# Packed attention with a SoLU layer: batch 1's Z from float16 halves, and a new order of steps after the first key product

## The chip, the core and the metric

The kernel runs on one core of a Trainium2 chip. The metric is the time of one execution in device microseconds (us), taken on the device; shown is the median of three timed runs. A profile is a separate execution, recorded instruction by instruction. Engines are called PE (TensorE, matrix products), DVE (VectorE), ACT (ScalarE), POOL (GpSimd) and SP (SyncE, which issues nearly all transfers here). PEld is the load of PE's stationary operand, which runs beside PE's products.

## The reference

There are 8 batches with 8 heads, 576 tokens, a head dimension of 64 and 32 packed rows. All tensors are float32.

```python
def sm_attn(qq, kk, vv):
    s = scale * np.matmul(qq, kk.transpose(0, 1, 3, 2))
    s = s - np.max(s, axis=-1, keepdims=True)
    a = np.exp(s)
    a = a / (np.sum(a, axis=-1, keepdims=True) + 1e-09)
    return np.matmul(a, vv)
p_packed = sm_attn(p, k, v)
out = sm_attn(q, p_packed, p_packed)

# x: out with the heads side by side, 4608 tokens x 512
h = x @ w_in                                    # 512 -> 1024
h_max = np.max(h, axis=-1, keepdims=True)
e = np.exp(h - h_max)
sm = e / (np.sum(e, axis=-1, keepdims=True) + 1e-09)
solu = h * sm
mu = np.mean(solu, axis=-1, keepdims=True)
var = np.mean((solu - mu) ** 2, axis=-1, keepdims=True)
ln = (solu - mu) / np.sqrt(var + 1e-06) * g_ln
return (ln @ w_out).astype(np.float32)          # 1024 -> 512
```

## The kernel before

**Flows and their order.** The program is written as generators, called flows, each of which emits its instructions step by step and yields in between. One long string, ORDER, names the flow that takes its next step. Every engine runs its instructions in the order in which they are emitted, so ORDER sets by hand what stands behind what on each engine and on SP's queue. The names in it: lp, lg, lw, lo, lk, lq, lv load p, g_ln, w_in, w_out, k, q, v; W and O take the sizes and scaled halves of w_in and w_out; Z and X issue PE products whose result nobody uses (warm_up, and keep_clock in pairs of L125 products); N, S, C, H are weight_size, w_out_scale, scaled_parts and weight_halves; k*b*, q*b*, z*b* are pack, unpack and make_z of batch *b*; t*i* is token_tile *i*.

**What a batch does.** Pack takes k and v to the packed rows: PE transposes or DVE block transposes of k (L369, L376, L383), scores (L399), maximum on DVE (L403), exponential e on ACT (L406), transposes of e on PE (L422) that are copied to SBUF as e1T (L424), the product with v (L432), and ppT, the packed rows transposed (L448). Unpack takes q to the attention weights a, in float16 halves a_h and a_l: scores (L504, L516), block transposes (L477), the softmax's maximum, difference, exponential, sum, reciprocal and product (L481 to L496), and the halves (L527, L530, L532). The attended rows are never formed: make_z multiplies the packed rows by w_in first, Z = packed rows times w_in, and splits Z into float16 halves zh and zl. Batches 0 and 1 do that in float32 (L570); batches 2 to 7 multiply halves of the packed rows (pph, L549 to L553) by halves of w_in (L564), three products in the place of one.

**What a token tile does.** 4608 tokens are 36 tiles of 128. An even batch and the odd one behind it have four tiles each and share one of the rest (tiles 4, 13, 22, 31). A tile is h = a times Z in 12 float16 products (L631), the negated maximum nm on DVE (L634), its scaled form on ACT (L639), a bound and s_row on POOL (L642 to L648), the exponential on ACT (L652), u = e times h on DVE (L656), negmu on ACT (L660), halves of u plus negmu on ACT (L665) and DVE (L667), a transposing transfer to yT on SP's queue (L670), the square on ACT (L673), small factors on POOL (L676 to L683), 24 output products (L691) and the scaled copy o_sb on ACT or DVE (L697, L699), which SP stores (L708).

**Space.** PSUM has three buffers h of two banks each, which score products, transposes, Z and the tiles' h take in turn, and one each of po and pa. There are three raw buffers for k and q, and one of v (v_sb). A product that takes a buffer waits until the reader of the one before it is done.

**Who does what.** Letter tables choose the engine, p for POOL, d for DVE, a for ACT, for one batch, piece or tile each: SCALED_BY the low part wcl of w_out's scaled halves (L305 to L313; g is POOL), A2L_BY a_l, SOFT_BY the difference and the product of the softmax, LOW_BY the low bits of the weights (L240 to L250), QT_BY and E1T_BY the copies of q's and e's transposes. ZP_BY says with 1 which batches make Z from halves. The line numbers here and in the rows are those of this kernel.

## Time and profile before

| | |
|---|---|
| median of three timed runs | 389.76 us (389.49 to 390.9) |
| profiled execution, own time | 390.44 us |
| its span, first to last instruction | 388.6 us |
| PE busy | 373.8 us, 96% |
| DVE busy | 294.3 us, 76% |
| ACT busy | 256.7 us, 66% |
| POOL busy | 244.8 us, 63% |
| mean granted PE clock | 0.995 |

The own time is 1.8 us longer than the span: that is what lies around the recorded instructions. The profiled execution is 0.68 us above the median. The shares are means over the whole span; the stages differ, so the views by stretch say more. "Idle before" in a row is the time in which the engine waited for the instruction, with what released it.

### The profile page before, as it was taken

The page shows a single profiled execution, that of the slowest core. Times are in us where ns is not written, and L with a number is a line of the kernel's source. Part 1 is how long each engine was busy: PE and PEld are TensorE (multiplying, and loading weights), DVE is VectorE, ACT ScalarE, POOL GpSimd, SP SyncE. Part 2 cuts the span into 40 slices and gives each one's busy share as a digit, 9 for nine tenths or more (in the row PEclk, how much of TensorE's full clock was granted, in tenths as well). Part 3 has the DMA queues.
Part 4 walks back from the last instruction along what each step waited for, and adds up shares of the span by engine and source line. Part 5 has one row for each costly group of instructions (what it writes and reads, how often), then busy time and mean ns, then how long its engine had stood idle before and what let it go on. Part 6 is the DMA issues. An engine that isn't in the chain of part 4 may idle for free.

```text
span 388.6 us, 8528 instructions
## 1 busy us (share of the span) xinstructions
PE 373.8 (96%) x3234; PEld 190.9 (49%) x3234; DVE 294.3 (76%) x472; ACT 256.7 (66%) x447; POOL 244.8 (63%) x410
## 2 busy tenths in 40 slices
PE   6978979999999999999999999999999999999996
PEld 6856435444545444544454455444444444444444
DVE  2577888999987987778798589977777968466631
ACT  2566799795878678955767657754658559465730
POOL 2674689887438987764555476875456658854550
PEclk9989999999999999999999999999999999999999
DMA  8999894898899999999697878873632435353561
GB/s 310 385 375 355 195 213 89 201 167 183 150 228 166 201 215 172 175 180 230 143 199 145 204 142 189 189 167 67 128 81 59 107 108 83 83 132 86 83 162 54
DMA packets 213017, 66.10 MB, mean 170 GB/s; under 512 B 192872, under 2 KB 206960, under 8 KB 212464
## 3 DMA queue, kind: packets, MB, share of 16 engines
q1 hardware_dynamic: 212976, 65.56, 74.4%
q8 instruction: 25, 0.41, 0.5%
q14 instruction: 16, 0.13, 0.1%
HBM read 37.23 MB, written 9.44 MB: 120 GB/s over the span
## 4 chain that ended last, share of the span: by engine, by line
PE 71%; DVE 4%; DMA 2%; ACT 1%; POOL 1%; issue 1%; SPq 0%; DVEq 0%; ACTq 0%
PE po L691 37%; PE h L631 19%; PE h L691 5%; PE h L564 2%; PE pa L432 2%; PE h L399 2%; PE h L516 1%; DMA yT<-yhl 1%; PE h L422 1%; DMA raw<-in_q_dram 1%; DVE u L656 1%; DVE w_in_sb L344 1%; DVE nm L634 1%; ACT e L652 1%; DVE s L477 0%
## 5 line engine op out<-in xcount | busy, mean ns | idle before, releaser
L691 PE MATMUL po<-wch,yT 128*128 128x512 f16 x512 | 160.1, 379 | 0.1
L691 PEld LDWEIGHTS <-yT 128*128 128x128 f16 x888 | 85.8, 98 | 100.6 <-issue 5.3
L691 PE MATMUL po<-wcl,yT 128*128 128x512 f16 x256 | 97.0, 379 | 0.0
L656 DVE SCALAR_TENSOR_TENSOR u<-e,s_row,h 128x1024 f32<-128x1024 f32 x36 | 45.8, 1271 | 18.3 <-ACT e L652 12.9
L667 DVE SCALAR_TENSOR_TENSOR yhl<-u,negmu,yhl 128x1024 f16<-128x1024 f32 x36 | 47.5, 1319 | 4.7 <-ACT yhl L665 4.6
L634 DVE TENSOR_REDUCE nm<-h 128x1 f32<-128x1024 f32 x36 | 43.5, 1212 | 8.3 <-PE h L631 7.9
L631 PE MATMUL h<-zh,a_h 128*128 128x512 f16 (+2 forms) x168 | 47.7, 380 | 0.7 <-ACT qT L371 0.7
L631 PE MATMUL h<-zl,a_h 128*128 128x512 f16 (+2 forms) x168 | 47.9, 380 | 0.0
L631 PEld LDWEIGHTS <-a_h 128*128 128x128 f16 (+2 forms) x336 | 27.7, 100 | 34.6 <-issue 5.2
L652 ACT ACTIVATE e<-h,nmc,z_scale 128x1024 f32<-128x1024 f32 x36 | 43.2, 1201 | 1.9 <-PE h L631 0.8
L665 ACT ACTIVATE yhl<-u,negmu 128x1024 f16<-128x1024 f32 x36 | 41.1, 1145 | 0.7
L673 ACT ACTIVATE e<-u,negmu 128x1024 f32<-128x1024 f32 x36 | 40.9, 1137 | 0.0
L639 ACT ACTIVATE nmc<-nm,z_scale 128x1 f32<-128x1 f32 x33 | 9.6, 292 | 45.9 <-DVE nm L634 45.9
L642 POOL TENSOR_SCALAR bound<-nm,z_scale 128x1 f32<-128x1 f32 x33 | 12.9, 390 | 37.6 <-DVE nm L634 36.1
L680 POOL TENSOR_SCALAR c_row<-sq,s_eps 128x1 f32<-128x1 f32 x36 | 12.8, 355 | 29.3 <-ACT e L673 26.4
L631 PE MATMUL h<-zh,a_l 128*128 128x512 f16 (+2 forms) x84 | 30.4, 379 | 0.1
L631 PE MATMUL h<-zl,a_l 128*128 128x512 f16 (+2 forms) x84 | 30.4, 379 | 0.0
L699 DVE TENSOR_SCALAR o_sb<-po,c_row,inv 128x512 f32<-128x512 f32 x18 | 14.6, 810 | 13.8 <-PE po L691 6.9
L681 POOL TENSOR_TENSOR c_row<-c_row,neg_half 128x1 f32<-128x1 f32 x36 | 22.5, 626 | 3.0
L660 ACT ACTIVATE negmu<-su 128x1 f32<-128x1 f32 x36 | 7.2, 200 | 25.5 <-DVE u L656 25.4
L496 POOL TENSOR_TENSOR a<-a,sm 128x576 f32<-128x576 f32 x16 | 20.3, 1274 | 4.9 <-DVE sm L494 4.3
L532 POOL TENSOR_TENSOR a_l<-s,a_h 128x576 f16<-128x576 f32 x14 | 20.4, 1460 | 4.5 <-ACT a_h L530 4.5
(173 smaller groups left out, 687.8 us busy)
## 6 DMA issues: line engine op xcount, KB each, us to landing
out_dram<-o_sb SPq DMA_DIRECT2D x34, 256.0 KB, 2.3
v_sb<-in_v_dram SPq DMA_DIRECT2D x8, 1024.0 KB, 8.3
raw<-in_k_dram SPq DMA_DIRECT2D x24, 288.0 KB, 4.4
raw<-in_q_dram SPq DMA_DIRECT2D x96, 72.0 KB, 2.5
zh<-in_moe_w_in_dram SPq DMA_DIRECT2D x2, 1024.0 KB, 8.0
zl<-in_moe_w_in_dram SPq DMA_DIRECT2D x2, 1024.0 KB, 7.9
raw<-in_k_dram SPq DMA_DIRECT2D x2, 1024.0 KB, 12.2
raw<-in_moe_w_out_dram SPq DMA_DIRECT2D x2, 1024.0 KB, 8.4
```

Of the source, the lines that this page charges most:

```text
L496: EN(nc, SOFT_BY[2 * b + 1]).tensor_tensor(out=w2, in0=w2, in1=sm.unsqueeze(2).broadcast_to([P, NB, J]), op=ALU.mult)
L532: EN(nc, A2L_BY[2 * b + r]).tensor_tensor(out=lo, in0=a2T, in1=hi, op=ALU.subtract)
L631: nc.tensor.matmul(dst_[:, cols], lhsT=lhsT, rhs=z[:, r, cols], start=bool(first), stop=bool(last))
L634: nc.vector.tensor_reduce(out=nm, in_=h, axis=AX.X, op=ALU.max, negate=True)
L652: nc.scalar.activation(e, h, AF.Exp, bias=nmc, scale=sc[:, 1:], accum_out=se)
L656: nc.vector.scalar_tensor_tensor(out=u, in0=e, scalar=s_row, in1=h, op0=ALU.mult, op1=ALU.mult, accum_out=su)
L665: nc.scalar.activation(yhl[:, 0], u, AF.Identity, bias=negmu)
L667: nc.vector.scalar_tensor_tensor(out=yhl[:, 1], in0=u, scalar=negmu, in1=yhl[:, 0], op0=ALU.add, op1=ALU.subtract)
L673: nc.scalar.activation(e, u, AF.Square, bias=negmu, accum_out=sq)
L681: nc.gpsimd.tensor_tensor(out=c_row, in0=c_row, in1=neg_half, op=ALU.pow)
L691: nc.tensor.matmul(po[:, cols], lhsT=yT[:, a, c], rhs=w[:, c, cols], start=c == 0 and t == 0, stop=c == NFC - 1 and t == 2)
L699: nc.vector.tensor_scalar(out=o_sb[:, cols], in0=po[:, cols], scalar1=c_row, scalar2=inv, op0=ALU.mult, op1=ALU.mult)
```

## The change

Five things change.

- ZP_BY: batch 1's Z is made from the float16 halves, like batches 2 to 7, with 48 float16 products in the place of 16 float32 ones. Its weight halves (H) must therefore be ready before z1, where they had to be ready before z2. The packed rows of batch 1 get halves as well.
- Tables: three of eight wcl parts go from POOL to DVE, a_l on DVE goes from two to seven of 16 pieces, softmax steps on DVE from two to eight of 32 (the table has now an entry for each half of a batch), three copies (two of e1T, one of q1) from ACT to DVE, and the low bits of O2 and O3 from ACT to POOL.
- warm_up yields between its products, which are the same and stand in the same place.
- weight_halves can put its subtraction on POOL; HL_BY puts all four on DVE, as before.
- ORDER is new from the first key product on. Among much else, three pairs of keep_clock's products stand behind the first token tile's h product, and q rows of batch 2 are loaded ahead of batch 1's v.

```diff
-SCALED_BY = 'gggggggg'
+SCALED_BY = 'ggdgdgdg'
-A2L_BY = 'ddpppppppppppppp'
-SOFT_BY = 'ppppppppdppppppp'
-LOW_BY = 'appapaaa'
+A2L_BY = 'pdpppdpddppdddpp'
+SOFT_BY = 'pppdpppppppppppdddppppdppdpdpppd'
+LOW_BY = 'appapapp'
...
-QT_BY = 'dadaaaaaaaaaaaa'
-E1T_BY = 'aaaaaa'
+QT_BY = 'dadaaaaaadaaaaa'
+E1T_BY = 'aaaaaaadaaadaaaa'
...
-ZP_BY = '00111111'
+ZP_BY = '01111111'
...
+HL_BY = 'dddd'
...
@@ warm_up @@
-        for _ in range(24):
-            nc.tensor.matmul(spare[:, :P], lhsT=ones_f, rhs=ones_f, start=True, stop=True)
...
-        yield
+        for _ in range(6):
+            for _ in range(4):
+                nc.tensor.matmul(spare[:, :P], lhsT=ones_f, rhs=ones_f, start=True, stop=True)
+            yield
...
@@ weight_halves @@
-            nc.vector.scalar_tensor_tensor(out=halves[1][g], in0=w_in_sb[:, g], scalar=s_w, in1=halves[0][g], op0=ALU.mult, op1=ALU.subtract)
+            if HL_BY[g] == 'd':
+                nc.vector.scalar_tensor_tensor(out=halves[1][g], in0=w_in_sb[:, g], scalar=s_w, in1=halves[0][g], op0=ALU.mult, op1=ALU.subtract)
...
@@ pack @@
-            copy_by(nc, E1T_BY[2 * b + i0 // 8] if b < 3 else 'a')(e1T[:, i0:i0 + len(grp)], pt[:, :len(grp) * P].rearrange('p (i j) -> p i j', j=P))
+            copy_by(nc, E1T_BY[2 * b + i0 // 8])(e1T[:, i0:i0 + len(grp)], pt[:, :len(grp) * P].rearrange('p (i j) -> p i j', j=P))
...
@@ unpack @@
-            EN(nc, SOFT_BY[2 * b]).tensor_tensor(out=s2[r], in0=s2[r], in1=mx.unsqueeze(2).broadcast_to([P, NB, J]), op=ALU.subtract)
+            EN(nc, SOFT_BY[4 * b + r]).tensor_tensor(out=s2[r], in0=s2[r], in1=mx.unsqueeze(2).broadcast_to([P, NB, J]), op=ALU.subtract)
...
-            EN(nc, SOFT_BY[2 * b + 1]).tensor_tensor(out=w2, in0=w2, in1=sm.unsqueeze(2).broadcast_to([P, NB, J]), op=ALU.mult)
+            EN(nc, SOFT_BY[4 * b + 2 + r]).tensor_tensor(out=w2, in0=w2, in1=sm.unsqueeze(2).broadcast_to([P, NB, J]), op=ALU.mult)
```

Of ORDER the diff is one line of some 1,290 steps, so three places of it are shown as the engines see them. Behind a name stands the number of its buffer. The lines of the kernel after are 4 higher than before up to weight_halves and 8 higher behind it.

PE ahead of the first token tile, before: the last two of z0's four product groups (L570), transposes of k1 and q1 (L369, L376), fillers (L125), the two score products of k1 (L399) and the first weight load of the tile.

```order
L570 MATMUL h_488<-w_in_sb_84,ppT_419 32x512 x4
L125 MATMUL po_120<-ones_98 128x384 x2
L376 MATMUL h_588<-ident_91,raw_470 128x128 x2
L125 MATMUL po_120<-ones_98 128x384 x2
L399 MATMUL h_597<-kT_509,pT_82 32x288 x8
L369 MATMUL h_622<-ident_91,raw_521 128x128 x8
L399 MATMUL h_642<-kT_509,pT_82 32x288 x8
L369 MATMUL h_661<-ident_91,raw_521 128x128 x8
L125 MATMUL po_120<-ones_98 128x384 x2
L631 LDWEIGHTS a_h0_116
L631 MATMUL h_672<-zh_486,a_h0_116 128x512
```

The same place after (L578 is z0's product, L377 and L384 are transposes, L129 the filler, L407 the score product, L639 the tile):

```order
L377 MATMUL h_551<-ident_91,raw_470 128x128 x8
L281 MATMUL pa_564<-ssq_89,ones_f_96 128x8
L384 MATMUL h_578<-ident_91,raw_470 128x128 x2
L129 MATMUL po_120<-ones_98 128x384 x2
L407 MATMUL h_597<-kT_509,pT_82 32x288 x8
L407 MATMUL h_614<-kT_509,pT_82 32x288 x8
L129 MATMUL po_120<-ones_98 128x384 x2
L377 MATMUL h_642<-ident_91,raw_631 128x128 x8
L377 MATMUL h_658<-ident_91,raw_631 128x128 x8
L639 LDWEIGHTS a_h0_116
L639 MATMUL h_667<-zh_489,a_h0_116 128x512
```

Both score products of k1 now stand next to each other, ahead of both transposes of q1, so that with three h buffers the tile's buffer is now that of the second score product (h_614) instead of a transpose of q1; one pair of fillers stands between them and none directly ahead of the tile.

VectorE in the same place, before: the maximum of k1's scores (L403), z0's splits (L580), a_l (L532) and a transpose of a (L527).

```order
L403 TENSOR_REDUCE nmx_613<-h_597 128x1
L580 SCALAR_TENSOR_TENSOR zh_486<-h_488,z_scale_465,zh_486 128x512
L231 TENSOR_SCALAR yhl_497<-e_544 128x1024
L532 TENSOR_TENSOR a_l0_118<-s2_610,a_h0_116 128x576
L336 TENSOR_SCALAR s_w_634<-w_size_456 128x1
L527 STREAM_TRANSPOSE s2_639<-a2_577 128x576
L403 TENSOR_REDUCE nmx_655<-h_642 128x1
L532 TENSOR_TENSOR a_l0_118<-s2_639,a_h0_116 128x576
L383 STREAM_TRANSPOSE kT_680<-raw_519 128x576 x2
L413 RECIPROCAL rs_685<-rs_685 128x2
```

The same place after (L295 and L296 are two of w_out's scale steps, L504 a softmax product, L535 and L540 the transpose and a_l, L588 the split of z0, L312 the wcl parts).

```order
L293 TENSOR_SCALAR up_572<-inv_87 128x1
L235 TENSOR_SCALAR yhl_528<-e_530 128x1024
L295 TENSOR_SCALAR gs_88<-g_sb_83,up_572 128x8
L296 TENSOR_SCALAR inv_87<-inv_87 128x1
L504 TENSOR_TENSOR a2_532<-a2_532,sm_547 128x576
L535 STREAM_TRANSPOSE s2_592<-a2_524 128x576
L411 TENSOR_REDUCE nmx_606<-h_597 128x1
L535 STREAM_TRANSPOSE s2_612<-a2_532 128x576
L588 SCALAR_TENSOR_TENSOR zh_489<-h_491,z_scale_465,zh_489 128x512
L411 TENSOR_REDUCE nmx_625<-h_614 128x1
L540 TENSOR_TENSOR a_l0_118<-s2_612,a_h0_116 128x576
L312 SCALAR_TENSOR_TENSOR wcl_86<-yhl_314,gs_88,wch_85 128x512
```

A softmax product and the last small steps of w_out's scale now stand ahead of the two maxima (L411), one a_l has left, and wcl parts follow.

SP's queue around the load of batch 1's v (v_sb_114), before:

```order
L153 DMA raw_519<-in_k_dram 32x72x32
L133 DMA raw_521<-in_q_dram 128x8x256
L147 DMA raw_521<-in_q_dram 32x2x128 x4
L153 DMA raw_519<-in_k_dram 32x72x32 x3
L133 DMA v_sb_114<-in_v_dram 128x8x256
L164 DMA v_sb_114<-in_v_dram 64x8x64
L153 DMA raw_748<-in_k_dram 32x72x32 x2
```

After:

```order
L157 DMA raw_587<-in_k_dram 32x72x32 x3
L137 DMA raw_631<-in_q_dram 128x8x256
L151 DMA raw_631<-in_q_dram 32x2x128 x4
L163 DMA raw_652<-in_q_dram 32x18x32 x4
L157 DMA raw_587<-in_k_dram 32x72x32
L163 DMA raw_652<-in_q_dram 32x18x32 x4
L137 DMA v_sb_114<-in_v_dram 128x8x256
L168 DMA v_sb_114<-in_v_dram 64x8x64
L163 DMA raw_727<-in_q_dram 32x18x32 x8
```

Eight issues of q rows of batch 2 (raw_652) now stand ahead of batch 1's v, in a buffer that k1 (raw_470) had, which PE transposes for the last time just ahead of the score products.

## Rows read from the trace of the kernel before

**Rows 1.** Stretches: us, busy (x count) PE, PEld, DVE, ACT, POOL; PEclk, DMA, GB/s
```profile
40.00:60.00 20.00, 17.27 (x132) 9.11 (x132) 17.70 (x37) 18.09 (x30) 15.14 (x16) 1.00 0.94 196
60.00:112.00 52.00, 51.69 (x568) 23.78 (x566) 49.42 (x81) 40.64 (x74) 39.08 (x63) 1.00 0.83 170
112.00:360.00 248.00, 247.78 (x2055) 118.68 (x2054) 192.44 (x305) 166.40 (x298) 160.26 (x287) 1.00 0.71 147
```

**Rows 2.** Waits of PE: engine, line, awaited; total us, times, longest us
```profile
PE h L691 <- DMA yT<-yhl: 0.6, 1, 0.6
PE h L399 <- DVE u L656: 0.2, 1, 0.2
```

**Rows 3.** Chain of waits from 141 us: start, us, what
```profile
141.65 5.18 PE po L691 x24
146.82 1.42 PE h L564 x48
```

**Rows 4.** Timeline of PE: start, us, line, out<-in, shapes, count
```profile
39.11 0.97 PE L125 MATMUL po<-ones 128*128 128x384 f32 x4
40.01 1.06 PE L570 MATMUL h<-w_in_sb,ppT 64*32 64x512 f32 x8
...
54.13 0.59 PE L631 MATMUL h<-zh,a_h 128*128 128x512 f16 x2 [0.68 <-ACT qT L371]
...
54.78 0.59 PE L631 MATMUL h<-zh,a_h 128*128 128x512 f16 x2
55.50 0.39 PE L631 MATMUL h<-zh,a_l 128*128 128x512 f16 x1
...
58.10 0.38 PE L631 MATMUL h<-zh,a_l 128*128 128x512 f16 x1
58.53 1.23 PE L422 MATMUL h<-ident,e 128*128 128x128 f32 x8
...
76.10 1.92 PE L570 MATMUL h<-w_in_sb,ppT 64*32 64x512 f32 x24
78.16 0.72 PE L399 MATMUL h<-kT,pT 64*32 64x288 f32 x16
78.67 1.06 PE L570 MATMUL h<-w_in_sb,ppT 64*32 64x512 f32 x8
79.67 0.39 PE L691 MATMUL po<-wch,yT 128*128 128x512 f16 x1
```

**Rows 5.** Timeline of VectorE (DVE), from 39 to 104 us
```profile
39.22 0.84 DVE L477 STREAM_TRANSPOSE s<-h 128x288 f32<-128x288 f32 x2
...
53.11 0.71 DVE L403 TENSOR_REDUCE nmx<-h 128x1 f32<-128x576 f32 x1
...
60.21 1.28 DVE L656 SCALAR_TENSOR_TENSOR u<-e,s_row,h 128x1024 f32<-128x1024 f32 x1 [0.42 <-ACT e L652]
...
102.26 1.27 DVE L667 SCALAR_TENSOR_TENSOR yhl<-u,negmu,yhl 128x1024 f16<-128x1024 f32 x1
```

**Rows 6.** Line L483 on VectorE: shortest, median, longest ns; first and last start
```profile
L483 DVE TENSOR_TENSOR s<-s,mx x2: 748/750/751, 181.8 to 182.4; 128x576 f32<-128x576 f32 x2
```

**Rows 7.** SP's issues and the landings of v_sb, yT (last number: median us)
```profile
47.83 1.45 SPq L133 DMA_DIRECT2D v_sb<-in_v_dram  x1
...
59.82 1.93 SPq L159 DMA_DIRECT2D raw<-in_q_dram  x4
...
DMA to landing us min/median/max: 5.8/7.9/8.8
...
yT<-yhl SPq DMA_TRANSPOSE x36, 3.9
```

**Rows 8.** Timeline of DVE, then POOL, at 88 us; line L532 by itself
```profile
89.06 2.30 DVE L667 SCALAR_TENSOR_TENSOR yhl<-u,negmu,yhl 128x1024 f16<-128x1024 f32 x1
...
88.40 4.11 POOL L532 TENSOR_TENSOR a_l<-s,a_h 128x576 f16<-128x576 f32 x2 [0.52 <-ACT a_h L530]
...
L532 POOL TENSOR_TENSOR a_l<-s,a_h x14: 1266/1280/2261, 88.4 to 333.2; 128x576 f16<-128x576 f32 x14
```

More of the change, by code (lines that the diff above doesn't have):

```diff
@@ L115, in warm_up @@
     def warm_up():
-        for _ in range(24):
-            nc.tensor.matmul(spare[:, :P], lhsT=ones_f, rhs=ones_f, start=True, stop=True)
-        for _ in range(15):
-            nc.tensor.matmul(spare, lhsT=ones, rhs=ones.unsqueeze(1).broadcast_to([P, DM // P, P]), start=True, stop=True)
-        yield
+        for _ in range(6):
+            for _ in range(4):
+                nc.tensor.matmul(spare[:, :P], lhsT=ones_f, rhs=ones_f, start=True, stop=True)
+            yield
+        for _ in range(5):
+            for _ in range(3):
+                nc.tensor.matmul(spare, lhsT=ones, rhs=ones.unsqueeze(1).broadcast_to([P, DM // P, P]), start=True, stop=True)
+            yield
     def keep_clock():
@@ L343, in weight_halves @@
             yield
-            nc.vector.scalar_tensor_tensor(out=halves[1][g], in0=w_in_sb[:, g], scalar=s_w, in1=halves[0][g], op0=ALU.mult, op1=ALU.subtract)
+            if HL_BY[g] == 'd':
+                nc.vector.scalar_tensor_tensor(out=halves[1][g], in0=w_in_sb[:, g], scalar=s_w, in1=halves[0][g], op0=ALU.mult, op1=ALU.subtract)
+            else:
+                nc.gpsimd.tensor_scalar(out=w_in_sb[:, g], in0=w_in_sb[:, g], scalar1=s_w, scalar2=0.0, op0=ALU.mult, op1=ALU.add)
+                nc.gpsimd.tensor_tensor(out=halves[1][g], in0=w_in_sb[:, g], in1=halves[0][g], op=ALU.subtract)
             yield
```

2 lines of the change are left out of this document (1 added, 1 removed).

## The prediction

> **What bounds the kernel now.** I read the stages first. The third column of [rows 1] is PE's busy time. In 40 to 60 us PE is busy 17.27 of 20 us while VectorE has 17.70 and ScalarE 18.09; PE still waits for operands there. From 60 to 112 us PE has 51.69 of 52 and VectorE 49.42 of 52, so both are full. From 112 to 360 us PE has 247.78 of 248 and VectorE only 192.44: PE alone sets the pace, at a granted clock of 1.00 (2.4 GHz). PE's waits, read next, say the same: after the first token tile the largest are 0.6 us for a transposed tile near the end and 0.2 us for VectorE's u [rows 2]. The chain of waits, read last, is PE's own work from there on, an output product of a tile as 24 rows in 5.18 us [rows 3].
>
> So the end is the moment at which the first token tile's h product starts (54.13 us, [rows 4]), plus PE's work from there, plus PE's pauses. Three kinds of change can move it: that start, the amount of PE work behind it, and pauses where VectorE is full (60 to 112 us). Work moved between VectorE, ScalarE and GpSimd after 112 us should be hidden by PE. The cover is the PE work between a tile's h product and its output product, in which the other engines treat that tile; for the last tile the new order has 72 output products of 0.216 us there, 15.5 us, and for no tile did I count less than 13.
>
> **The change part by part.** The sum is made on the profiled execution, 390.44 us with a span of 388.6. The median of the three timed runs, 389.76, lies 0.68 lower, so I add the differences to the median.
>
> *Batch 1's Z.* Now: float32 products from 76.10 to 78.16 and again from 78.67 to 79.67, 3.06 us of PE [rows 4]. After: 48 float16 products, as batches 2 to 7 have them, 1.42 us [rows 3]. PE is full there, so this is worth **-1.64 us**. What it adds (the packed halves of ppT) and the eight weight-half operations, which must now be done before z1, lie on VectorE and ScalarE; they come back below as VectorE's load.
>
> *Fillers.* The clock-keeping products (L125) were all issued before the first token tile; three pairs now stand behind its h product. Two pairs take 39.11 to 40.01, 0.45 us a pair [rows 4]. If PE is full where they now stand that is **+1.35 us**; if PE would have waited there anyway, 0. I take the full price, since by the chain below their successors' operands are ready.
>
> *The start of the first token tile.* Before, it waited for a bank that a copy of q1 freed (0.68 us, [rows 4]). In the new order its bank is that of batch 1's second score product, so it waits for VectorE's second L403 and ScalarE's exponential behind it. I followed VectorE's new order by hand from the common point, the second L477 [rows 5], with durations of rows of the same form, each instruction starting about 0.07 us before the one ahead has ended. O3's L250 goes behind the second z0 split and ends at 44.3; the two sums end at 45.0 and 46.4 and the second reciprocal at 47.05, 1.0 us earlier than before. Then come S's eight small steps (1.5 us), the third z0 split, O3's shift, and the softmax product of one half, which moved here from GpSimd (0.75 us, as the same form on VectorE, [rows 6]): 50.8. A transpose, L403, a transpose, the last z0 split and the second L403 follow: 54.1, where before that L403 ended at 53.82 [rows 5]. The exponential takes 1.0 us and starts behind a wch step at 54.2, so the tile starts at about 55.2: **+1.05 us**. Bounds: 0, if ScalarE is a little quicker than I followed it, to +2.2, if each of its waits costs 0.2 us more. O2's and O3's low bits, moved from ScalarE to GpSimd, I price at nothing: GpSimd waits for VectorE's shift of O2 at that time; without that wait they would cost it about 1.5 us each.
>
> *Pauses that go.* Two products from 54.78 are fed by 55.21, the next starts at 55.50: 0.29 us. A product of 58.10 is fed by 58.32, the transposes start at 58.53: 0.2 us [rows 4]. 0.2 us and 0.6 us are in the list of waits [rows 2]. In the new order the first tile has its operands and the last output products stand far behind their h products: **-1.3 us**. Bounds 0 to -1.3.
>
> *Pauses that come.* (a) Tile 1 takes the bank of batch 1's e1T copy, which ScalarE reaches only after two q1 copies; followed by hand that copy ends at 59.8 while PE is there at 59.2: **+0.6**. (b) On SP's queue batch 1's v now stands behind q rows of batch 2, whose buffer is free only when PE has read the last of k1 (about 48.8). With 1.93 us for four q issues it is issued at about 53.3 instead of 47.83, and lands 5.8 to 8.8 us later [rows 7], at 59 to 63 with its second piece; PE wants it at 62.4. I take 0; bounds 0 to +1.5. (c) VectorE between the first tile's u (ended 61.49) and tile 4's second half (ended 103.53) [rows 5]: 59 instructions that are 37.9 us of work by the means of their forms, so 4.1 us were lost. The new order has 65 there, 39.2 us; up to tile 5's second half it has 49.5 us against 44.4, because transposes of batch 3, its two L403 and tile 6's u now go first. With the same share lost, 5.3 us, tile 5's half is ready at 62.6 + 54.8 = 117.4, is transposed 3.9 us later [rows 7] at 121.3, and PE wants it at about 120.5: **+0.8**. Bounds 0 (nothing lost) to +3.9 (below).
>
> *What moves off GpSimd.* Eleven softmax and a_l steps of 0.75 us, three wcl parts of about the same, the packed pieces and three small copies are some 12 us more on VectorE and 18 us less on GpSimd. Most of it lies after 112 us, where VectorE has 55.6 us of idle time; there I price it at 0. Without that cover it would be up to 9 us.
>
> Sum: -1.64 + 1.35 + 1.05 - 1.3 + 0.6 + 0.8 = **+0.86 us**, a span of 389.5 and a median of 390.6: no change that can be told (0.5%, 1.95 us, is about what a measurement of this kernel can tell from none).
>
> **The rivals.** *Faster: the new order was better informed than my chain.* The start does not move (-1.05), PE would have waited where the fillers stand (-1.35), and neither new pause shows (-1.4): 390.6 - 3.8 = **386.8**. For it: the fillers stand just ahead of tile 0's output product, whose transposed rows PE may well be too early for. Against: the fillers, the start and the pauses must come out well together. Below 387.8: 0.21.
>
> *Slower: VectorE and GpSimd block each other, and VectorE stalls PE.* At 89.06 a VectorE L667, 1.27 us at 102.26 [rows 5], took 2.30, while two GpSimd a_l steps, usually 1.28 each, took 4.11 over the same stretch [rows 8]: one stood still while the other worked. The weight halves now come at 68 to 71 us instead of 80 to 105, where GpSimd has its wcl parts back to back, and three wcl parts on VectorE come at 55 to 57. Three collisions as at 89.06 are 3 x 1.03 = 3.1 us on VectorE: tile 5's rows land at 124.4 against 120.5, a pause of 3.9 in the place of 0.8, **393.7**. It decides from the point at which VectorE loses more than 4.5 us between 62.6 and 116.6 us. For it: VectorE is busy 95% of 60 to 112 us. Against: VectorE's work there was hit once at full length. With v landing late on top it is 395. Above 391.7: 0.29.
>
> The Trainium skill, "SBUF — State Buffer", section "Who interferes with whom", says that a VectorE instruction with two SBUF inputs and a GpSimd instruction that reads SBUF exclude each other for the whole instruction; the trace agrees, by 1.03 us at 89.06. By that rule the later moves to VectorE take away partners on GpSimd as well, so only the early ones should hurt, as this rival has it.
>
> *The change does not do what it says:* the order shows batch 1's products as float16 in one place, so I give that nothing.
>
> **How the numbers follow.** The forecast, within 0.5% of 389.76 (387.8 to 391.7), has 0.50, its own range 389.0 to 391.7. Faster 0.21, slower 0.29. The range 387.3 to 393.8 leaves out about 0.08 of the faster cases and 0.11 of the slower ones. The predicted time is 390.6.
>
> **What would show it.** In the profile after: the first L631 product between 54.5 and 56.5 us, waiting for the exponential; 1.4 us for batch 1's Z in the place of 3.06; PE's waits after the first tile 1 to 2.5 us in all, at tile 1 and at a transposed tile around 120 us; VectorE about 306 us busy and GpSimd about 227; PE full after 125 us. A PE pause of over 2 us between 60 and 125 us that names VectorE or a transposed tile is the slower rival. PE waits of over 2 us after 130 us would show the cover argument wrong, and a first tile before 54 us the chain that I followed by hand.

## The result, and the profile after

The kernel after takes 395.64 us (median of 4 runs, 394.79 to 397.0); the kernel before, run beside it, 389.84. The ratio is 1.0147, 95% interval [1.0111, 1.0184]: **slower by 1.5%, 5.8 us**, where 390.6 was forecast, and outside the range that was given (387.3 to 393.8).

The profiled execution of after has an own time of 394.79 us and a span of 393.0, 4.4 us more than the span of before. The other 1.4 us lie between profile and median: after's median is 0.85 above its own profile, before's 0.6 below. Busy times first (busy us, share of the span, instructions):

```profile
PE 374.1 (95%) x3250; PEld 190.9 (49%) x3250; DVE 305.7 (78%) x491; ACT 254.8 (65%) x443; POOL 228.1 (58%) x395
```

VectorE at 306 and GpSimd at 228 us are what was forecast, and PE's busy time has hardly moved (373.8 before). So the loss is time in which PE stands still or gets through its work more slowly. The stretches of after, to be held against [rows 1] (us, busy and count of PE, PEld, DVE, ACT, POOL, granted PE clock, DMA share, GB/s):

```profile
40.00:60.00 20.00, 15.79 (x126) 9.83 (x119) 18.76 (x38) 17.00 (x29) 12.42 (x11) 0.91 0.90 199
60.00:112.00 52.00, 51.14 (x585) 23.81 (x584) 49.42 (x86) 40.87 (x74) 36.76 (x64) 1.00 0.86 172
112.00:360.00 248.00, 246.72 (x2043) 116.98 (x2042) 200.90 (x316) 166.09 (x295) 146.44 (x272) 1.00 0.71 144
```

Two things are new. In 40 to 60 us the granted clock is 0.91 where it was 1.00. And from 112 us on, where PE was without a gap, 1.06 us of busy time are missing. PE's waits of after, to be held against [rows 2] (engine, line, awaited; total us, times, longest):

```profile
PE h L377 <- ACT kT L379: 2.0, 1, 2.0
...
PE po L699 <- DMA yT<-yhl: 0.8, 3, 0.4
PE h L407 <- issue: 0.8, 1, 0.8
...
PE h L699 <- DVE o_sb L707: 0.7, 1, 0.7
PE h L639 <- ACT e1T L432: 0.7, 1, 0.7
```

Waits say where PE stood, not how far it fell behind, since a wait can swallow an earlier gain. So I worked out of both traces, product by product, how much later after has the same PE work left (each form of product has one price in both; the fillers and batch 1's Z, which differ, count nothing). The first tile starts 0.24 us later. At 75 us after lies about 2.2 us behind, at 125 us 1.0, at 210 us 1.6, at 225 us 3.4, at 360 us 3.8, at the end 4.4.

**Up to 125 us the forecast sum of +0.86 came out; the loss is what came behind it**: 1.8 us at one place at 215 us, 0.6 at the end, and 1.1 in small pieces. The place at 215 us, on PE's timeline (start, us, line, out<-in, shapes, count, idle before and releaser):

```profile
211.43 0.41 PE L572 MATMUL h<-w_hi,pph 64*32 64x512 f16 x8
...
212.52 0.40 PE L572 MATMUL h<-w_hi,pph 64*32 64x512 f16 x8
212.85 1.32 PE L440 MATMUL pa<-v_sb,e1T 128*32 128x64 f32 x80
214.11 0.68 PE L407 MATMUL h<-kT,pT 64*32 64x288 f32 x7
215.56 0.69 PE L407 MATMUL h<-kT,pT 64*32 64x288 f32 x9 [0.77 <-issue]
216.18 0.33 PE L446 MATMUL pa<-ident,pp 128*128 128x128 f32 x1
```

The last products of the same Z group and the score group, with the 80 products elsewhere, as before has them:

```profile
212.14 0.40 PE L564 MATMUL h<-w_hi,pph 64*32 64x512 f16 x8
212.36 0.67 PE L399 MATMUL h<-kT,pT 64*32 64x288 f32 x16
212.96 0.33 PE L438 MATMUL pa<-ident,pp 128*128 128x128 f32 x1
```

A score group of 16 takes 0.60 us to the next start there. In after its first 7 need 1.45 and the other 9 need 0.62: 1.5 us are lost in the middle of a group that had already started. The profile names no releaser ("issue"); what the traces say of it comes with the experiments.

The end of after, PE's timeline again:

```profile
385.36 0.27 PE L699 MATMUL h<-wch,yT 128*128 128x256 f16 x1
386.33 0.27 PE L699 MATMUL h<-wch,yT 128*128 128x256 f16 x1 [0.69 <-DVE o_sb L707]
```

The last tile's two halves stand back to back in one buffer, so that the second waits until VectorE has copied the first out.

### The profile page after: what moved, and what is told of

Its sections match the earlier page's. It is cut to its first block, busy times and chain, and to the rows that moved or that the text cites. A ratio compares the mean times of both kernels' runs of the same rounds, so it can differ in the third digit from the quotient of the medians.

```text
span 393.0 us, 8527 instructions
## 1 busy us (share of the span) xinstructions
PE 374.1 (95%) x3250; PEld 190.9 (49%) x3250; DVE 305.7 (78%) x491; ACT 254.8 (65%) x443; POOL 228.1 (58%) x395
## 4 chain that ended last, share of the span: by engine, by line
PE 82%; DMA 5%; DVE 4%; ACT 3%; SPq 3%; issue 1%; POOL 1%; DVEq 0%; ACTq 0%
PE po L699 40%; PE h L639 21%; PE h L699 5%; DMA yT<-yhl 5%; PE h L430 2%; PE po L119 2%; PE h L572 2%; PE h L407 2%; SPq L163 2%; PE pa L440 2%; PE h L377 1%; PE h L524 1%; PE h L213 1%; SPq L157 1%; PE po L123 1%
## 5 line engine op out<-in xcount | busy, mean ns | idle before, releaser
L639 PE MATMUL h<-zh,a_h 128*128 128x512 f16 (+2 forms) x168 | 47.7, 380 | 0.8 <-ACT e1T L432 0.7
L639 PE MATMUL h<-zl,a_h 128*128 128x512 f16 (+2 forms) x168 | 47.7, 380 | 0.0
L639 PEld LDWEIGHTS <-a_h 128*128 128x128 f16 (+2 forms) x336 | 27.7, 100 | 34.4 <-issue 4.2
L639 PE MATMUL h<-zl,a_l 128*128 128x512 f16 (+2 forms) x84 | 30.3, 379 | 0.0
L639 PE MATMUL h<-zh,a_l 128*128 128x512 f16 (+2 forms) x84 | 30.3, 379 | 0.0
L504 POOL TENSOR_TENSOR a<-a,sm 128x576 f32<-128x576 f32 x11 | 13.8, 1262 | 16.9 <-DVE sm L502 13.0
L639 PEld LDWEIGHTS <-a_l 128*128 128x128 f16 (+2 forms) x168 | 14.3, 99 | 16.8
L689 POOL TENSOR_TENSOR c_row<-c_row,neg_half 128x1 f32<-128x1 f32 x36 | 20.0, 556 | 3.0
L656 POOL TENSOR_TENSOR s_row<-bound,neg_one 128x1 f32<-128x1 f32 x33 | 19.7, 595 | 2.8
L699 PE MATMUL h<-wch,yT 128*128 128x512 f16 (+1 forms) x80 | 20.5, 336 | 0.7 <-DVE o_sb L707 0.7
```

Source lines behind the costliest of these rows:

```text
L504: EN(nc, SOFT_BY[4 * b + 2 + r]).tensor_tensor(out=w2, in0=w2, in1=sm.unsqueeze(2).broadcast_to([P, NB, J]), op=ALU.mult)
L639: nc.tensor.matmul(dst_[:, cols], lhsT=lhsT, rhs=z[:, r, cols], start=bool(first), stop=bool(last))
L656: nc.gpsimd.tensor_tensor(out=s_row, in0=bound, in1=neg_one, op=ALU.pow)
L689: nc.gpsimd.tensor_tensor(out=c_row, in0=c_row, in1=neg_half, op=ALU.pow)
L699: nc.tensor.matmul(po[:, cols], lhsT=yT[:, a, c], rhs=w[:, c, cols], start=c == 0 and t == 0, stop=c == NFC - 1 and t == 2)
```

## The experiments

Four theories stood against each other: (1) the loss begins ahead of the first tile, in the places of the fillers and of ScalarE's copy of kT, and in the clock; (2) batch 1's Z in float16, with the VectorE steps that it needs early, gives no time back; (3) the work moved off GpSimd costs more on VectorE than it frees; (4) the loss is a handful of single waits that the order makes late. A letter in a quoted expectation stands for one of these; its sentence says which. In the diffs a line is a piece of ORDER. The runs are from several chips; each ratio is against runs of the kernel before on the same chip. "..." marks what is left out of a diff.

### Fillers and the first tile

*Three pairs of fillers back ahead of the first tile* (a_fill_back).

```diff
-z0 z0 k1 q0 k1 S
+z0 z0 k1 q0 X X X k1 S
...
-H t0 H C7 X C7 q1 t1
+H t0 H C7 C7 q1 t1
...
```

> The kernel after, with the three pairs of clock-keeping products that stand behind the first token tile's h product (1.7 us of PE work there) put ahead of k1's second transposes, where PE stood idle for 2.04 us. Theory A, the fillers stand in the wrong place (their price behind the first tile is full, and the clock falls to half for 3.3 us behind the idle stretch that they left): PE's wait there shrinks to 0.7 us, the granted clock of 45 to 50 us stays at 1.00, the mean clock goes from 0.991 or less to 0.995, and the median falls by 1.7 us for the work and about 1 us more for the clock, to about 392.9. Rival B, PE would have waited behind the first tile anyway, since VectorE or GpSimd are late there: the pauses grow by what the fillers gave up and the median stays within 0.7 us of 395.6.

395.89 us (394.79 to 397.07, 5 runs), 1.0156 [1.0133, 1.0180]: no gain. The first tile starts at 53.06, 1.3 us earlier than in after. PE then stands at batch 1's v, which it had reached so late in after that 0.2 us of waiting were left:

```profile
61.97 0.77 PE L440 MATMUL pa<-v_sb,e1T 128*32 128x64 f32 x40 [1.36 <-DMA v_sb<-in_v_dram]
```

Its distance behind before is 3.6 us at 225 us, where after's is 3.4. The fillers' places are not where 5.8 us went.

*ScalarE's copy of kT ahead of q0's exponential* (a_kT_first), to take away the 2.0 us wait of after's list.

```diff
-q0 q0 q0 X O3 O3 q0 q0 z0 z0 k1 q0 k1
+q0 q0 k1 q0 X O3 O3 q0 q0 z0 z0 q0 k1
```

> The kernel after, with ScalarE's copy of k1's first transposes ahead of the first exponential of batch 0's softmax, so that PE's second transposes of k1 need not wait 2.04 us for it. Theory A1, that late copy is what costs: the first tile starts 1 to 2 us earlier and the median falls by as much. Theory A2, VectorE's chain to the second maximum sets the start of the first tile, and PE's idle time only moves: the first tile still starts at 54.4 plus or minus 0.4, PE waits some 3 us ahead of q1's transposes instead, and the clock's fall moves there, to about 51 to 55 us, where it costs the first tile up to 1.6 us; the median lies between 395 and 397.

397.71 us (396.73 to 398.69, 4 runs), 1.0201 [1.0178, 1.0223]. The wait was replaced by a longer one behind it, and the clock fell for longer (0.83 in 40 to 60 us):

```profile
48.70 0.60 PE L281 MATMUL pa<-ssq,ones_f 128*128 128x8 f32 x2 [2.82 <-DVE ssq L290]
```

*Four more pairs of fillers*, on top of a_fill_back (a_clock), so that PE has no gap at 44 to 46 us. The clock of after in three stretches (columns as above), then that of a_clock:

```profile
44.00:46.00 2.00, 0.21 (x2) 0.21 (x3) 1.30 (x3) 1.96 (x6) 1.39 (x2) 0.99 0.73 194
46.00:48.00 2.00, 2.00 (x11) 2.00 (x10) 1.56 (x7) 1.57 (x4) 0.38 (x1) 0.50 1.08 367
48.00:50.00 2.00, 2.00 (x36) 1.06 (x35) 1.90 (x8) 1.55 (x3) 0.62 (x1) 0.66 0.36 74
```

```profile
44.00:46.00 2.00, 1.90 (x12) 1.58 (x11) 1.32 (x3) 1.96 (x5) 1.41 (x2) 1.00 0.62 167
46.00:48.00 2.00, 1.53 (x13) 1.21 (x11) 1.70 (x9) 2.00 (x4) 0.38 (x1) 1.00 1.07 378
48.00:50.00 2.00, 1.89 (x37) 0.94 (x36) 1.97 (x7) 1.42 (x4) 0.93 (x1) 1.00 0.48 103
```

In after PE is idle for nearly all of 44 to 46 us and then runs at 0.50 (1.2 GHz) and 0.66; with fillers in the gap it keeps 1.00 (2.4 GHz).

> The kernel after with the three filler pairs ahead of k1's second transposes, two more pairs there and two more ahead of q1's transposes, so that PE stands idle for less than 0.4 us at a time between 38 and 54 us. If idle time there is what makes the granted clock fall a second time (46 to 50 us in the kernel after, never there in before): the clock stays at 1.00 from 32 us on, and the first tile starts where before's did with the same clock ahead of 32 us, 53.3 to 54.1. If that is what the medians of the kernel after pay over its profile: the median falls by about 1, to 394.6; if VectorE and the load of v take it back, as in a_fill_back, it stays at 395.6 to 396.

```diff
-z0 z0 k1 q0 k1 S
+z0 z0 k1 q0 X X X X X k1 S
...
-k1 lq1 C3 C4 X q1 C6
+k1 lq1 C3 C4 X X X q1 C6
...
```

395.27 us (393.42 to 398.92, 6 runs), 1.0139 [1.0101, 1.0177]; span 391.6. By the traces it is 1.4 us better than after; the medians do not tell them apart.

*The fillers of after in the kernel before* (b_fill).

```diff
-q0 k1 z0 X z0 S q0
+q0 k1 z0 z0 S q0
...
-q1 q1 lq2 C7 t3 t1 t0
+q1 q1 lq2 C7 X t3 t1 t0
...
```

> The kernel before, with three of its filler pairs (those of 42.69, 46.60 and 52.86 us) moved to where the new order has them, behind the first tile's h product: that part of the change alone. If the fillers' place is what the change pays for: PE's work behind the first tile grows by 1.7 us and the granted clock falls a second time, between 43 and 55 us; the median rises by 1.7 to 3.3, to 391.4 to 393. If PE's fillers behind the tile are hidden by other waits, as a_fill_back made it look in the new order: the median stays within 0.7 us of 389.7.

391.43 us (390.46 to 392.24, 12 runs), 1.0010 [0.9990, 1.0029]: in the order of before, PE's work behind the first tile grows by 1.5 us and the median by less than can be told. The profiled execution shows nearly the full price: its span is 390.1 us, 1.4 more than before's, although the first tile starts earlier (53.66). The two do not agree; that execution, 391.83 us, is among the longer of the twelve. There is no second fall of the clock (granted 1.00 in 40 to 60 us).

### Batch 1's Z

*Z in float32 in the order of after* (a_z1_f32).

```diff
-ZP_BY = '01111111'
+ZP_BY = '00111111'
...
-t3 t3 t2 k2 z1 q1 q1 q1
+t3 t3 t2 k2 q1 q1 q1
...
-t1 q1 k2 k2 H z1 t2 z1
+t1 q1 k2 k2 z1 z1 z1 t2 z1
...
```

> The kernel after, with batch 1's Z from float32 products as before and the last seven steps of the weight halves behind it: the change of Z alone undone, everything else as after. If Z from halves is worth its PE work because PE is full there: PE's work behind the first tile grows by 1.3 us (2.92 us of float32 products in the place of 1.65), the waits stay, and the median rises by 1.3, to about 396.9. If what it adds to VectorE (the weight halves early) is what made the pauses: the pauses between 70 and 145 us, 1.2 us in all, vanish, and the median stays at 395.6 or falls.

401.50 us (400.40 to 402.19, 4 runs), 1.0295 [1.0274, 1.0317]. The 32 records of the float32 products, now side by side, take 1.9 us, not 2.9. But the weight halves, which I put behind them, delay VectorE elsewhere, so this says little of Z's own worth:

```profile
88.33 1.95 PE L578 MATMUL h<-w_in_sb,ppT 64*32 64x512 f32 x32
...
105.61 0.56 PE L462 MATMUL pa<-total,ones_f 128*128 128x1 f32 x2 [3.98 <-DVE ppT L456]
```

*Z in float16 in the order of before* (b_z16): ZP_BY as in after, H's steps 3 to 9 pulled ahead of the products that need them, the last two z1 steps behind t1's.

```diff
-ZP_BY = '00111111'
+ZP_BY = '01111111'
...
-q2 t2 z1 t2 H q1 z1 k2 t3 t1 z1 q1
+q2 t2 H z1 t2 H H q1 H k2 H t3 t1 H q1
...
```

> The kernel before, with batch 1's Z from float16 halves and the four weight halves ahead of it (four steps of 1.25 us on VectorE, three of 1.14 us on ScalarE pulled forward to 80 us), its products behind tile 1's output products. PE's work falls by 1.5 us. If VectorE has no room there, as a_z1_f32 made it look: PE waits 2 to 4 us between 85 and 105 us, for batch 1's a_l or a transposed tile, and the median rises by 0.5 to 2.5. If it has room: the median falls by 1.5, to 388.2.

393.02 us (390.98 to 394.48, 12 runs), 1.0045 [1.0020, 1.0069]. PE has 1.3 us less work and three new waits of 4.3 us in all, one for a transposed tile and two for VectorE's and ScalarE's steps that the halves pushed back:

```profile
77.59 0.39 PE L691 MATMUL po<-wch,yT 128*128 128x512 f16 x1 [1.75 <-DMA yT<-yhl]
84.20 0.40 PE L564 MATMUL h<-w_in_sb,pph 64*32 64x512 f16 x5 [0.72 <-DVE w_in_sb L344]
87.28 1.23 PE L422 MATMUL h<-ident,e 128*128 128x128 f32 x8 [1.81 <-ACT e L406]
```

*The float32 Z of before, merely put side by side* (b_zadj): a gain for PE that costs VectorE nothing.

```diff
-t2 H q1 z1 k2 t3 t1 z1 q1 lq3
+t2 H q1 z1 z1 k2 t3 t1 q1 lq3
```

> The kernel before, with the last of the four float32 product groups of batch 1's Z moved ahead of the score products that stood between: all 32 records side by side. In the kernel before they took 1.92 us for 24 and 0.99 for the last 8 alone; side by side in a_z1_f32 32 took 1.88. If products on the two halves of the rows run beside each other: batch 1's Z takes 1.9 us and the median falls by 1.0, to 388.7, so that float16 halves were worth only 0.5 us here. If not: Z takes 2.6 or more, and the median stays within 0.5 of 389.7.

391.58 us (390.23 to 393.01, 12 runs), 1.0016 [0.9994, 1.0037]. PE saves 0.8 us (one row of 2.14 in the place of 1.92 + 1.06 in [rows 4]) and gives it back at once:

```profile
75.45 2.14 PE L570 MATMUL h<-w_in_sb,ppT 64*32 64x512 f32 x32
...
93.05 0.39 PE L631 MATMUL h<-zl,a_h 128*32 128x512 f16 x2 [1.55 <-DVE zl L580]
```

The zl that it waits for stood on VectorE behind two instructions that took 2.3 us each:

```profile
87.27 2.32 DVE L344 SCALAR_TENSOR_TENSOR w_in_sb<-w_in_sb,s_w,w_hi 128x1024 f16<-128x1024 f32 x1
89.51 2.29 DVE L667 SCALAR_TENSOR_TENSOR yhl<-u,negmu,yhl 128x1024 f16<-128x1024 f32 x1
91.72 1.27 DVE L580 SCALAR_TENSOR_TENSOR zl<-h,z_scale,zl 128x1024 f16<-128x1024 f32 x1
```

Only one of the two is new: L667 took 2.30 us in before too [rows 8], L344 took 1.24 there. So zl starts 0.44 us later than in before (91.28), and PE, whose last product ahead of it started at 91.11 instead of 92.17, is 1.06 us earlier; the two make the wait.

*The same with that wait mended* (b_best: H's step and k3's first step moved behind the last z1 step), and *with the next one mended too* (b_best2: t3's transposing transfer ahead of the last issues of q's third load).

```diff
-q1 z1 t2 k2 k3 q1 t1 q1
+q1 z1 t2 k2 q1 t1 q1
...
-q1 t2 t3 z1 q1 t4 k3
+q1 t2 t3 z1 H k3 q1 t4 k3
...
```

> The kernel before with b_zadj's edit (batch 1's Z in one piece, 0.84 us less PE work) and, on VectorE, the fifth step of the weight halves and one k transpose (2.0 us together) moved behind the last split of batch 1's Z, for which PE waited 1.55 us in b_zadj. If VectorE's order alone ate the gain there: no wait for that split, and the median falls by 0.8 to 1.5 against before, a version ahead of both kernels. If something else is next on VectorE: a wait of about 1 us for a transposed tile or a later k piece between 95 and 115 us, and the median stays within 0.5 of before.

> The kernel before with b_best's edits, and tile 3's transposing transfer issued on SP as soon as its rows are ready (89 us), ahead of the last quarter of a q load and of an output store that stood before it there until 94.2 us; in b_best PE waited 1.60 us for those rows. If that is the last thing between the work saved on batch 1's Z (0.84 us) and the end: the wait goes, the length behind the first tile falls by 0.8 to 1.6 against before, and the median by 0.8 to 1.2, a version ahead of both kernels. If VectorE hands it on once more (the q piece that now comes later, or the tiles behind): the median stays within 0.5 of before.

390.11 us (389.14 to 392.04, 12 runs), 0.9998 [0.9982, 1.0015], and 391.46 us (389.69 to 393.34, 12 runs), 1.0043 [1.0022, 1.0064]. Each mended wait is followed by another. In b_best it is a transposed tile, whose transfer SP issued only behind eight loads of q and a store (its rows were ready at 89.0); in b_best2 it is VectorE again. First b_best, PE and then SP's queue, then b_best2:

```profile
99.73 0.39 PE L691 MATMUL po<-wch,yT 128*128 128x512 f16 x1 [1.60 <-DMA yT<-yhl]
```

```profile
89.01 4.51 SPq L159 DMA_DIRECT2D raw<-in_q_dram  x8
...
94.17 2.11 SPq L670 DMA_TRANSPOSE yT<-yhl  x1
```

```profile
99.57 0.33 PE L438 MATMUL pa<-ident,pp 128*128 128x128 f32 x1 [1.15 <-DVE pp L435]
```

*VectorE alone made longer, in the kernel before* (b_dve_plus): tile 2's maximum is taken twice; nothing else differs and the result of the maximum is the same.

```diff
+        if i == 2:
+            nc.vector.tensor_reduce(out=nm, in_=h, axis=AX.X, op=ALU.max, negate=True)
```

> The kernel before, with the maximum of tile 2 taken twice on VectorE (1.21 us more work at 68 us, same result): the price of VectorE time in the stage of 60 to 112 us by itself. If only PE's work and pauses count there, as my prediction's bound had it: the median rises by 0.3 or less. If VectorE is as critical as PE there: PE's pauses between 68 and 112 us grow by about 1 us, for a transposed tile or a split of Z, and the median rises by 0.8 to 1.2.

390.99 us (389.77 to 391.99, 12 runs), 1.0026 [1.0012, 1.0039]: **1.2 us more on VectorE cost 1.0 us** (0.5 to 1.5 by the interval), while PE is busy 51.69 of the 52 us of that stretch [rows 1]. The added row on VectorE, and PE's next wait:

```profile
69.35 1.23 DVE L636 TENSOR_REDUCE nm<-h 128x1 f32<-128x1024 f32 x1
```

```profile
71.48 0.72 PE L399 MATMUL h<-kT,pT 64*32 64x288 f32 x16 [0.66 <-DVE s L477]
```

### Work moved off GpSimd

*Tables nearly as before, order of after* (a_engines): a_l, softmax, wcl and copies go back to GpSimd and ScalarE, except in batch 0.

```diff
-SCALED_BY = 'ggdgdgdg'
-A2L_BY = 'pdpppdpddppdddpp'
-SOFT_BY = 'pppdpppppppppppdddppppdppdpdpppd'
+SCALED_BY = 'gggggggg'
+A2L_BY = 'pdpppppppppppppp'
+SOFT_BY = 'pppdppppppppppppddpppppppppppppp'
...
```

> The kernel after, in its order, with the steps behind batch 0 back on the engines that did them before: three wcl parts, five a_l and the softmax steps on GpSimd, the copies of e1T and q1 on ScalarE. If VectorE is overloaded or blocked by GpSimd in the kernel after: the pauses that name a transposed tile or VectorE (0.18, 0.25, 0.35 and 0.28 us) vanish, and the median falls by 1 us or more. If PE's work hides the move, as the prediction had it: the median stays within 0.7 us of 395.6, with GpSimd some 17 us busier and VectorE some 11 us less.

399.25 us (398.36 to 400.58, 4 runs), 1.0243 [1.0220, 1.0267]: 3.6 us slower than after. It falls 6.7 us further behind before between 125 us and the end, where after falls 3.4 further behind. So in this order the moves to VectorE help, and theory (3) falls.

### The places behind 125 us

*The late waits one by one* (a_waits): a_fill_back's fillers, v ahead of q's rows, t15's output products ahead of k5's and k6's products at 215 us, and the last tile's two halves parted by six products of tile 34.

```diff
-C4 X q1 C6 lq2 q1 q1
+C4 X q1 C6 lv1 lq2 q1 q1
...
-t35 t35 t34 t34 t35 t35 t34 t34 t35 t35 t35 t35 t35 t35
+t35 t35 t34 t35 t35 t35 t34 t34 t34 t35 t35 t35 t35 t35
```

> The kernel after with four places mended in its order: the three filler pairs ahead of k1's second transposes (as in a_fill_back), batch 1's v issued ahead of the q rows of batch 2, six output products of tile 15 ahead of pack 5's product with v and six ahead of its neighbour's first score product (where PE paused some 0.8 to 1.5 us in the middle of a group, at 215 us), and the last tile's two halves apart, with tile 34's last six products between them. If these waits are what holds PE: against a_fill_back (395.9) the wait for v (1.36 us), the pause at 215 us (about 1.4) and the wait at the end (0.69) go, and the median is about 392.5. If VectorE's order is the bound from 60 to 145 us: the wait for v turns into waits for VectorE and for transposed tiles of the same size, and the median is about 393.8.

397.56 us (395.30 to 400.41, 6 runs), 1.0175 [1.0126, 1.0224]. The waits for v and at the end are gone. At 215 us my edit made it worse, because t15's rows were not transposed yet:

```profile
216.15 0.39 PE L699 MATMUL po<-wch,yT 128*128 128x512 f16 x1 [1.94 <-DMA yT<-yhl]
```

This run also had no second fall of the clock (1.00 in 40 to 60 us), with the fillers of a_fill_back, which had one (0.91).

*A part of z4 moved away from 215 us* (a_split_z), and *q's load ahead of v's there* (a_sp), so that VectorE's transposes behind pp need not wait 1.5 us for raw.

```diff
-q4 q4 z4 t16 t14 t14 t17 z4 k5
+q4 q4 z4 t16 z4 t14 t14 t17 k5
```

> The kernel after, with the first 24 of batch 4's 48 Z products ahead of tile 14's last six output products, in the place of behind them, so that the short instructions of Z, of pack 5's product with v and of the next scores no longer run in one piece at 211.4 to 214.8 us; nothing else moves. If that dense stretch is what PE pauses for in the middle of a group at 215 us (0.77 in the trace of after, 1.1 to 1.6 in its relatives): the pause shrinks below 0.3 us and the step of 1.75 us at 210 to 225 us, by which the kernel after falls behind, goes; the median falls by 1 to 1.7. If the pause has another cause: it stays where it is in the program, and the median stays.

> The kernel after, with the last quarter of q5's load issued ahead of batch 5's v instead of behind tile 15's transposing transfer, which takes SP 5.9 us to issue behind that v. If SP's queue is what makes the place at 215 us late: VectorE's wait for that load (1.47 us) goes, the copy of ppT behind it comes 1.5 us earlier, the step by which after falls behind between 210 and 225 us shrinks from 1.75 to below 0.8, and the median falls by 0.5 to 1. If PE's pause there is its own: the step stays at 1.2 or more and the median stays within 0.5 of 395.6.

a_split_z: 396.19 us (394.13 to 396.96, 5 runs), 1.0158 [1.0134, 1.0183]; span 392.3. a_sp: 396.26 us (395.50 to 397.80, 6 runs), 1.0175 [1.0151, 1.0199]. With the dense run of products broken up, the stop in the score group is gone (16 in one row) and 0.5 us of another wait takes its place; with the load mended, the stop stays (1.43 us idle; after's second trace, the run below, has 1.20). First a_split_z, then a_sp:

```profile
213.36 1.32 PE L440 MATMUL pa<-v_sb,e1T 128*32 128x64 f32 x80 [0.52 <-DVE e1T L432]
214.65 0.89 PE L407 MATMUL h<-kT,pT 64*32 64x288 f32 x16
```

```profile
214.88 0.68 PE L407 MATMUL h<-kT,pT 64*32 64x288 f32 x7
217.00 0.69 PE L407 MATMUL h<-kT,pT 64*32 64x288 f32 x9 [1.43 <-issue]
```

So the stop at 215 us is not SP's queue seen through VectorE. Nor does the run of 48 + 80 + 16 short products make it alone: in a_clock and in a_z1_f32 the run stands as in after, and the group has no stop inside. First a_clock, then a_z1_f32:

```profile
211.70 1.32 PE L440 MATMUL pa<-v_sb,e1T 128*32 128x64 f32 x80
213.37 0.72 PE L407 MATMUL h<-kT,pT 64*32 64x288 f32 x16 [0.35 <-PE pa L440]
```

```profile
220.06 1.32 PE L440 MATMUL pa<-v_sb,e1T 128*32 128x64 f32 x80
221.32 0.72 PE L407 MATMUL h<-kT,pT 64*32 64x288 f32 x16
```

The traces point to a cause that no run was made to test: **PE waited for its own instructions.** One of the DMA queues that the profile calls "instruction", q8, moves 25 pieces of 16 KB in a run, about one for every 260 recorded instructions of PE (products, weight loads and semaphore steps). Six traces have the stop (after, its second trace, a_fill_back, a_kT_first, a_engines, a_sp). In each it comes behind exactly 4,033 of these instructions, and it ends 1.3 to 1.6 us after the end of such a transfer. In after the transfer lasts from 213.04 to 214.01 and the stop ends at 215.56; in a_sp it lasts from 214.56 to 215.49 and the stop ends at 217.00. a_clock has eight products of fillers more ahead, 16 instructions with their weight loads, so that the 4,033 end in front of the group. There PE is idle for 0.35 us, although the u whose bank the group takes had ended at 212.78, and its next instruction (213.26) comes 1.4 us after the end of such a transfer, an earlier one (210.88 to 211.82). A dense run uses up instructions fastest, which would be why the stop shows there. The transfer of a_engines, which starts at 218.59 and ends at 219.58, where the stop ends at 220.89 (218.5 to 219.0 us: packets, MB, share of 16 engines):

```profile
q8 instruction: 1, 0.02, 12.4%
```

Distances gained between 210 and 225 us: after 1.8, a_split_z 1.1 to 1.4, a_sp 2.4, a_clock 1.6. In a_clock a wait of 0.81 us for VectorE's ppT, at 217.75, takes most of the stop's place.

*After again*, for the spread from run to run.

> The kernel after, unchanged, for a second trace. Its median lay 0.85 us above its own profile, before's 0.6 below. If the granted clock alone makes the runs differ: this profile's span differs from 393.0 by no more than the difference in time lost to the clock before 58 us (0 to 6.8 us of half clock, up to 2.7 us of start), and behind the first tile both traces lose the same, 334.7 us plus or minus 0.4. If chance elsewhere does (VectorE and GpSimd standing in each other's way, transfers landing late): the length behind the first tile differs by 1 us or more, at places that can be named.

395.34 us (394.84 to 397.50, 4 runs), 1.0151 [1.0124, 1.0178]. The places are the same: 1.7 us behind at 75, 0.7 at 125, 1.2 at 210, 3.4 at 225, 4.5 at the end.

*All mendings that worked, together* (a_sum): a_clock's fillers, a_split_z, one step of k5 ahead of t14's last step there, a_sp's load, a_waits' end.

```diff
-q4 z4 t16 t14 t14 t17 z4 k5 z4 lq6
+q4 z4 t16 z4 t14 k5 t14 t17 z4 lq6
...
```

> The kernel after with the repairs of single places together: a_clock's fillers (its profile lay 1.4 us below after's), a_split_z's (0.7 us), the small e1T copy of batch 5 ahead of an o_sb on VectorE (0.5 us of PE's wait in a_split_z), the last quarter of q5's load ahead of batch 5's v on SP (VectorE waits 1.5 us for it, and PE 0.8 us for the ppT behind it in a_clock), and the last tile's halves apart (0.7 us). If the loss is a sum of such places, the profile comes to about 389.5 us of span, 3.5 below after's, and the median to 392 or less. If a place mended only hands its time to the next one, as in a_fill_back and a_waits, the span stays above 391 and the median above 394.

393.37 us (391.15 to 394.69, 6 runs), 1.0082 [1.0056, 1.0109]; span 389.4, 0.7 above before. The score group at 215 us runs through:

```profile
211.73 1.32 PE L440 MATMUL pa<-v_sb,e1T 128*32 128x64 f32 x80
213.28 0.72 PE L407 MATMUL h<-kT,pT 64*32 64x288 f32 x16 [0.23 <-DVE u L664]
```

It is 0.4 us ahead of before at 125 us and 1.1 behind at 225. The mendings take back 2.3 of the 5.8 us by the medians, and 3.6 of 4.4 by the profiled executions, where a_clock's fillers alone take back 1.4. No kernel of these beats the one before; b_best equals it.

## Why the prediction was wrong

**The step that failed is the cover.** Under "What moves off GpSimd" the prediction priced everything behind 112 us at 0, because VectorE has idle time there and PE sets the pace. Its own mark for that, PE waits of over 2 us after 130 us, was just missed in the list of waits and passed in lost time: behind 130 us PE's waits of over 0.1 us are 0.35, 0.11, 0.77 and 0.69, 1.9 us in all, but the stop at 215 us took 1.5 where the list has 0.77. The distance to before grew by 3.4 us from 125 us on. What filled it was not VectorE's added work (a_engines shows that it helps) but **places of the new order**: the stop in a dense run of short products at 215 us (with a little beside it 1.8 us; most likely PE's supply of instructions), the last tile's halves back to back (0.6), and small waits. The cover tells when operands are ready. I took it to mean that PE then runs without a pause: I had counted the products of a tile's cover for each tile, and not looked at what stands next to what on PE.

**The sum up to 125 us came out in part by luck.** The first tile came 0.8 us under its term, the fillers 0.35 over, and what is left for the pauses, those that go and those that come, is about +0.6 where +0.1 was forecast; these cancel. Term by term:

- *The first tile*: forecast +1.05, came +0.24, within the bounds. The chain was the right one: the tile waits for the second exponential, which starts at 53.44 against 54.2 forecast, since VectorE ended 0.7 us earlier. What I did not see is that PE has a gap of 2.0 us ahead of k1's second transposes, whose bank waits for ScalarE's copy of kT, and that the clock falls for a second time there:

```profile
45.79 1.85 PE L377 MATMUL h<-ident,raw 128*128 128x128 f32 x8 [2.04 <-ACT kT L379]
...
52.37 1.97 PE L377 MATMUL h<-ident,raw 128*128 128x128 f32 x16 [1.48 <-ACT e L414]
54.37 0.59 PE L639 MATMUL h<-zh,a_h 128*128 128x512 f16 x2
```

- *Fillers*: +1.35 forecast, 1.7 in PE's work behind the first tile. The full price was right in kind.
- *Z*: -1.64 forecast; PE's work shrinks by 1.5 (2.92, summed over the same records, to 1.42). In after it is time as well: the distance, in which Z counts nothing, falls by 1.2 us between 75 and 125 us. But that holds in this order alone. In the order of before the same edit gives nothing (b_z16), nor does a saving that costs VectorE nothing (b_zadj, b_best, b_best2), and 1.2 us more on VectorE cost 1.0. **"PE is full there, so this is worth -1.64 us" was no argument**: [rows 1] shows VectorE with 49.42 of 52, and two engines in turn set the pace.
- *Pauses*: those named went. Tile 1's wait for e1T was forecast at 0.6 and is 0.66. For v 0 was taken, with 1.5 as a bound; it is 0.2 in after, and 1.36 where PE came earlier (a_fill_back). Tile 5's +0.8 did not come: its transfer was issued at 116.91, where the forecast had its rows ready at 117.4, and PE had no wait for it (0.4 in after_again).

**The rivals.** The slower one had nearly the right time, 393.7, and not the mechanism. It wanted more than 4.5 us lost on VectorE between 62.6 and 116.6 us, and a stall at tile 5. By the prediction's own count VectorE did lose that: from the end of the first u (62.03) to tile 5's half (116.84) are 54.8 us, for 49.5 of work. But PE waited for no transposed tile between 110.7 and 143.6 us, and after shows only one collision of its kind in that stretch, 0.9 us:

```profile
82.86 2.18 DVE L675 SCALAR_TENSOR_TENSOR yhl<-u,negmu,yhl 128x1024 f16<-128x1024 f32 x1
```

The rule that was weighed there, of the Trainium skill, "SBUF — State Buffer", section "Who interferes with whom", is still borne out in size by b_zadj, where L667 took 2.29 us while GpSimd ran an a_l; it was not what decided here. The faster rival has nothing for it but the small start of the first tile.

**The last 1.4 us** come from carrying a difference of profiled executions over to medians. Eleven runs of before agree within 1.8 us on the chip where those of a_sum spread over 3.5, three of them at the same granted clock (0.996) over 2.0 (391.15 to 393.12). On another chip 29 runs of before spread over 5.1, so the spread is not the new order's alone.

**What stays open.** Whether PE's stop within the score group is the supply of instructions: the count and the times of the transfers say so, and no run was made to test it; a_split_z, a_sum, a_clock and a_z1_f32 show that it goes when the run is broken up and also when something else shifts against it. Why the clock fell a second time in a_fill_back and not in a_waits, with the same fillers. Why runs spread at one clock, and with that the last 2.2 us between a_sum's profile and its median. And the small pieces of after's loss, about 1 us between 125 and 360 us, were not taken apart, beyond 0.35 us for a transposed tile at 143.58.

## What to carry to other kernels

Where two engines are both nearly full in a stretch (here 99% and 95%), do not price a saving on one of them as time: put the same number of microseconds on the other as a test, and follow each mended wait to the next. Where work is reordered, look beyond what an engine's load allows: go through the rows of the bounding engine for dense runs of short instructions (a stop inside one may end just behind a transfer of the "instruction" queue), for a buffer reused back to back, and for gaps in which its clock can fall. Take the distance to the kernel before at several moments, and not the list of waits alone: it shows at once which stretch holds the loss.

## What the runs showed of the hardware

- In the middle of a group of 16 products PE lost 1.5 us in after and 2.1 in a_sp (0.77 and 1.43 of it shown as idle, "issue") behind a run of 48 + 80 short products. In all six traces with such a stop it ended 1.3 to 1.6 us after a 16 KB transfer in the queue "instruction". With the run broken up (a_split_z), or with 16 PE instructions more ahead of it (a_clock), there was no stop inside the group.
- 32 float32 records of Z take 1.9 to 2.1 us side by side (a_z1_f32, b_zadj), and 2.9 us as 24 + 8 with another group between them (before).
- After 2 us of idle PE the granted clock was 0.50 for the next 2 us and 0.66 for the two behind (after); with fillers in the gap it stayed at 1.00 (a_clock).
